# Transposing x into spare columns of the value banks, with a new order of loads and of work, in a fused window-attention and highway-layer kernel

## The chip, the cores and the metric

The kernel runs on one core of one Trainium2 chip. The metric is the device time of one execution in microseconds (us). Every timing below is a set of executions on one chip, with the kernel before run on the same chip in the same rounds. An execution is called slow when it is over 1.5% above the fastest of its kernel. The span of the profile is some 2 us shorter than the time of the same execution, so spans are compared with spans and times with times.

## The reference, cut to what matters

```python
# q, k, v: (4 batches, 8 heads, 768 positions, 64); first 4 positions are sinks, window of 128
scores = scale * q @ k.T
keep   = (pos_k < 4) | (0 <= pos_q - pos_k < 128)
a      = softmax(where(keep, scores, -1e9))
x      = (a @ v), heads side by side          # 3072 tokens x 512
H      = max(x @ w_h, 0)
T      = sigmoid(x @ w_t + b_t)
out    = T * H + (1 - T) * x
```

## The kernel before

The 3072 tokens are 24 blocks of 128. For each block TensorE does these steps, whose names are those of the order string further down: `S`, the scores (with the transposes of a later block's q and k ahead of them); `sk`, the scores against the four sinks, for one block or for two at once; `A`, the attention sums; `X`, the transposes of the result x; `Mh` and `Mt`, the two matrix products of the highway layer (hidden and gate). ScalarE does exp (`x0_`, `x1_`, `es`), tanh (`u`) and copies (`tq`, `tk`, `xT`). VectorE masks (`m0_`, `m1_`), normalises (`xh`) and combines (`d`, `e`, `o`); a `V` at the end of a copy's name means that VectorE does it. A step's place in the string is its place in the queue of its engine.

The accumulator memory has 8 banks: two tiles of two banks for scores (`s_ps`), one tile of two banks for attention sums, the value banks (`av_ps`), and two single work banks (`m_ps`), which `sk`, `X`, `Mh` and `Mt` take in turn.

```python
s_ps  = tc.tile_pool(name="ps_s",  bufs=2, space=PSUM)
av_ps = tc.tile_pool(name="ps_av", bufs=1, space=PSUM)
m_ps  = tc.tile_pool(name="ps_m",  bufs=2, space=PSUM)
...
def av_tile(n):
    if n not in av_of:
        av_of[n] = av_ps.tile([P, 2, 4, P], FP32, tag="av", name="av")   # 66 of each 128 columns used
    return av_of[n]
...
def pe_X(n):
    xh = xh_of[n]
    xtp = m_ps.tile([P, NOC, P], FP16, tag="m", name="xtp")              # a work bank
    for j in range(NOC):
        nc.tensor.transpose(xtp[:, j, :], xh[:, j * P:(j + 1) * P], ident)
    xtp_of[n] = xtp

def act_X(n, eng=None):
    xT = x_pool.tile([P, NOC, P], FP16, tag="xT", name="xT")
    (eng or nc.scalar.copy)(out=xT, in_=xtp_of.pop(n))
    xT_of[n] = xT
...
def pe_O(n):                                   # the sum of the last blocks' output, by TensorE
    ops = m_ps.tile([P, DM], FP32, tag="m", name="ops")
    nc.tensor.matmul(ops, lhsT=ident2, rhs=xh_of.pop(n), start=True, stop=False)
    nc.tensor.matmul(ops, lhsT=ident, rhs=ee_of.pop(n), start=False, stop=True)
    t_of[n] = ops
...
# GpSimd's queue of loads that cast to fp16
load_q(1); load_q(2); load_q(3); load_k(2)
...                                            # two small operations for a mask
load_k(4); load_k(3); load_v(2); load_w(moe_w_h, wh_sb); load_k(5); load_v(3)
load_w(moe_w_t, wt_sb); load_q(4); load_q(5)
...
ORDER = """
...
Mh:10 x1_:13 xh:12 Mt:11 tq:15 d:10 tk:15 m1_:13 X:12 u:11 S:14 xTV:12
e:10 A:13 x0_:14 o:10 Mh:11 x1_:14 xh:13 Mt:12 tq:16 d:11 tk:16 m0_:14 X:13 u:12 m1_:14 S:15
xT:13 e:11 sk:15 x0_:15 o:11 A:14 es:15 ...
...
"""
```

The softmax here doesn't subtract the row's maximum and nothing guards it: scores larger than these inputs give would overflow.

## Time and profile before

| | before |
|---|---|
| first timing, median of 3 runs | 126.18 us (126.16 to 127.13) |
| profiled execution | 126.71 us, span 124.6 us, granted TensorE clock 1.00 |
| TensorE busy | 112.2 us, 90% of the span |
| VectorE, ScalarE busy | 102.0 us, 91.5 us |

TensorE is the bound, VectorE comes next. I read a block's place in time from where its score step begins, that is from the first matmul of line 323, which has the same line in both kernels.

### The profile page before, as it was taken

To read this page: it belongs to the slowest core of one execution; us is meant where nothing else is said; L and a number is where in the kernel's file an instruction comes from. 1 tells how busy PE (TensorE), PEld (TensorE's weight loads), DVE (VectorE), ACT (ScalarE), POOL (GpSimd) and SP (SyncE) were. 2 spreads that over 40 slices of the span, in tenths; PEclk is the share of its full clock that TensorE was granted. 3 is DMA by queue.
4 is the path that set the end of the run, shared out by engine and by line. 5 is a ranking of instruction groups with operands and counts; after the bars stand their busy time and mean duration, and the time that the engine had idled before them with its cause. 6 is when DMAs were issued, how large, how long until landed. Compare 5 with 4: busy or idle time off the path is not lost.

```text
span 124.6 us, 4770 instructions
## 1 busy us (share of the span) xinstructions
PE 112.2 (90%) x2016; PEld 69.2 (56%) x2016; DVE 102.0 (82%) x239; ACT 91.5 (73%) x153; POOL 73.1 (59%) x97
## 2 busy tenths in 40 slices
PE   5958588999999979999999999999999999998950
PEld 1323356556675645766666666655665676663620
DVE  6855253889978999989998999799999999993970
ACT  2156478578899948889889699888798897953260
POOL 5998957799697899999599999642000000000000
PEclk9999999999999999999999999999999999999999
DMA  3999999999999999999999999996022211012044
GB/s 75 199 166 152 181 179 182 158 152 119 188 193 171 189 170 179 185 155 169 189 223 134 195 154 205 196 183 152 5 89 84 84 63 34 35 49 84 5 170 166
DMA packets 79847, 17.65 MB, mean 142 GB/s; under 512 B 75601, under 2 KB 76881, under 8 KB 79826
## 3 DMA queue, kind: packets, MB, share of 16 engines
q0 software_dynamic: 71888, 9.97, 127.1%
q1 hardware_dynamic: 6882, 7.11, 18.9%
q10 hardware_dynamic: 1056, 0.26, 1.3%
q8 instruction: 16, 0.26, 0.9%
q14 instruction: 5, 0.04, 0.1%
HBM read 21.01 MB, written 6.29 MB: 219 GB/s over the span
## 4 chain that ended last, share of the span: by engine, by line
PE 63%; DVE 20%; DMA 6%; issue 3%; POOL 2%; ACT 2%; DVEq 0%
PE tps L419 12%; PE hps L432 11%; DMA ksd<-in_k_dram 6%; PE av L378 6%; PE av L367 5%; DVE e L349 5%; PE sps L280 5%; DVE xh L397 4%; PE sps L323 4%; PE sps L336 4%; PE xtp L406 4%; PE tps L417 3%; PE sk L305 3%; PE av L384 3%; DVE ee L444 3%; DVE dd L438 3%
## 5 line engine op out<-in xcount | busy, mean ns | idle before, releaser
L341 ACT ACTIVATE e<-sps,ebias 128x768 f16<-128x768 f32 x48 | 41.1, 894 | 9.0 <-PE sps L336 9.0
L349 DVE TENSOR_TENSOR e<-e,mask 128x768 f16<-128x768 f16 x48 | 26.3, 570 | 4.4 <-ACT e L341 3.9
L285 ACT COPY t<-sps 128x512 f16<-128x512 f16 x45 | 24.1, 582 | 3.1 <-PE sps L280 3.1
L104 POOL DMA_DIRECT2D v<-in_v_dram x26 | 22.3, 860 | 5.9 <-DVE e L349 2.2
L432 PE MATMUL hps<-wh_sb,xT 128*128 128x512 f16 x92 | 23.4, 379 | 0.3 <-ACT u L425 0.3
L419 PE MATMUL tps<-wt_sb,xT 128*128 128x512 f16 x92 | 23.6, 379 | 0.0
L97 POOL DMA_DIRECT2D ksd<-in_k_dram x26 | 22.6, 874 | 0.4 <-issue 0.4
L90 POOL DMA_DIRECT2D qsd<-in_q_dram x23 | 21.4, 933 | 1.5 <-DMA qsd<-in_q_dram 1.2
L425 ACT ACTIVATE u<-tps 128x512 f16<-128x512 f32 x23 | 13.7, 597 | 7.3 <-PE tps L419 6.6
L397 DVE TENSOR_TENSOR xh<-av,rec 128x512 f16<-128x512 f32 x24 | 16.6, 692 | 0.8
L438 DVE SCALAR_TENSOR_TENSOR dd<-hps,xh 128x512 f16<-128x512 f32 x23 | 15.7, 688 | 1.8 <-PE hps L432 1.8
L444 DVE SCALAR_TENSOR_TENSOR ee<-u,dd 128x512 f16<-128x512 f16 x23 | 15.8, 687 | 0.8 <-ACT u L425 0.2
L450 DVE SCALAR_TENSOR_TENSOR otok<-xh,ee 128x512 f32<-128x512 f16 x20 | 14.5, 726 | 0.5
L419 PEld LDWEIGHTS <-xT 128*128 128x128 f16 x92 | 9.0, 98 | 9.8 <-issue 0.2
L432 PEld LDWEIGHTS <-xT 128*128 128x128 f16 x92 | 8.7, 98 | 7.6 <-issue 0.7
L323 PE MATMUL sps<-t,t 64*128 64x128 f16 x192 | 12.0, 217 | 0.2 <-ACT t L285 0.2
L367 PE MATMUL av<-v,e 64*64 64x66 f16 x384 | 10.9, 193 | 0.3 <-issue 0.2
L406 PE MATMUL xtp<-ident,xh 128*128 128x128 f16 x96 | 9.2, 219 | 2.0 <-DVE dd L438 1.0
L406 PEld LDWEIGHTS <-xh 128*128 128x128 f16 x96 | 6.8, 98 | 7.0 <-DVE xh L397 2.5
L378 PE MATMUL av<-v,e 128*128 128x66 f16 x192 | 10.4, 195 | 0.0
L392 DVE RECIPROCAL rec<-av 128x8 f32<-128x8 f32 x24 | 4.9, 204 | 5.9 <-PE av L384 5.2
L367 PEld LDWEIGHTS <-e 64*64 64x64 f16 x384 | 8.4, 107 | 1.9 <-issue 0.8
(84 smaller groups left out, 148.8 us busy)
## 6 DMA issues: line engine op xcount, KB each, us to landing
out_dram<-otok SPq DMA_DIRECT2D x23, 256.0 KB, 5.1
qsd<-in_q_dram POOLq DMA_DIRECT2D x23, 128.0 KB, 6.8
ksd<-in_k_dram POOLq DMA_DIRECT2D x19, 128.0 KB, 7.0
v<-in_v_dram POOLq DMA_DIRECT2D x19, 128.0 KB, 7.1
wh_sb<-in_moe_w_h_dram POOLq DMA_DIRECT2D x1, 512.0 KB, 8.1
wt_sb<-in_moe_w_t_dram POOLq DMA_DIRECT2D x1, 512.0 KB, 9.2
ksd<-in_k_dram POOLq DMA_DIRECT2D x7, 64.0 KB, 7.7
v<-in_v_dram POOLq DMA_DIRECT2D x7, 64.0 KB, 6.7
```

The lines of the kernel that those rows point to most:

```text
L90: nc.gpsimd.dma_start(out=qsd, in_=q[b, :, c * P:(c + 1) * P, :].transpose([1, 0, 2]))
L97: nc.gpsimd.dma_start(out=ksd[rows], in_=k[b, :, s0:s0 + nr, :].transpose([1, 0, 2]))
L104: nc.gpsimd.dma_start(out=vt[rows, :, 0:D], in_=v[b, :, s0:s0 + nr, :].transpose([1, 0, 2]))
L285: (eng or nc.scalar.copy)(out=t.rearrange("p a (h b) -> p h a b", b=HP), in_=t_view(s_tile(n, g), isinstance(n, tuple) and n[1:] in F32_T))
L341: nc.scalar.activation(out=e.rearrange("p a b c -> p a (b c)"), in_=s_tile(n, g)[:, :, 0:2 * EW], func=AF.Exp, bias=ebias, scale=SCALE)
L349: nc.vector.tensor_tensor(out=ev, in0=ev, in1=m.unsqueeze(1).to_broadcast([P, 4, EW]), op=ALU.mult)
L367: nc.tensor.matmul(av[part, h // 4, h % 4, 0:_AVN], lhsT=e_at(n, h)[src, P:EW], rhs=vt[src, 65 * h:65 * h + _AVN], start=(h % 4 == 0), sto ...
L397: nc.vector.tensor_tensor(out=xh.rearrange("p (h d) -> p h d", d=D), in0=av_of.pop(n)[:, :, 0:D], in1=rec_of.pop(n).unsqueeze(2).to_broadc ...
L406: nc.tensor.transpose(xtp[:, j, :], xh[:, j * P:(j + 1) * P], ident)
L419: nc.tensor.matmul(tps, lhsT=xT[:, kc, :], rhs=wt_sb[:, kc, :], start=False, stop=(kc == NOC - 1))
L432: nc.tensor.matmul(hps, lhsT=xT[:, kc, :], rhs=wh_sb[:, kc, :], start=(kc == 0), stop=(kc == NOC - 1))
L444: nc.vector.scalar_tensor_tensor(out=ee, in0=u_of.pop(n), scalar=1.0, in1=dd_of.pop(n), op0=ALU.add, op1=ALU.mult)
```

## The change

Its intent, in four parts.

1. x is transposed with eight transposes of 64 rows, into columns of the value banks that the attention sums leave unused. The work banks then serve `sk`, `Mh` and `Mt` alone.
2. A new order of the middle: the gate product before the hidden one, sink scores mostly behind the attention step, copies of x mostly on ScalarE.
3. A new start: another order of loads, made for the times at which they land, and another order of work.
4. A new tail, in which VectorE does all output sums.

```diff
-        load_q(1)
-        load_q(2)
         load_q(3)
         load_k(2)
+        load_q(4)
+        load_q(1)
+        load_k(3)
+        load_q(2)
+        load_v(2)
+        load_k(5)
 ...
         load_k(4)
-        load_k(3)
-        load_v(2)
+        load_v(3)
         load_w(moe_w_h, wh_sb)
-        load_k(5)
-        load_v(3)
-        load_w(moe_w_t, wt_sb)
-        load_q(4)
         load_q(5)
         load_k(6)
+        load_w(moe_w_t, wt_sb)
 ...
+    def x_view(n):
+        return av_t[n].bitcast(FP16)[:, :, :, 2 * _AVN:2 * _AVN + HP]
+
     def pe_X(n):
         xh = xh_of[n]
-        xtp = m_ps.tile([P, NOC, P], FP16, tag="m", name="xtp")
+        xv = x_view(n)
         for j in range(NOC):
-            nc.tensor.transpose(xtp[:, j, :], xh[:, j * P:(j + 1) * P], ident)
-        xtp_of[n] = xtp
+            for hf in range(2):
+                rows = slice(HP * hf, HP * hf + HP)
+                nc.tensor.transpose(xv[:, hf, j, :], xh[rows, j * P:(j + 1) * P],
+                                    ident[rows, rows])
 ...
-        (eng or nc.scalar.copy)(out=xT, in_=xtp_of.pop(n))
+        (eng or nc.scalar.copy)(out=xT.rearrange("p a (h b) -> p h a b", b=HP), in_=x_view(n))
 ...
-    H0 = 4
+    H0 = 3
 ...  (ORDER: all lines; two blocks of the middle)
-    Mh:10 x1_:13 xh:12 Mt:11 tq:15 d:10 tk:15 m1_:13 X:12 u:11 S:14 xTV:12
-    e:10 A:13 x0_:14 o:10 Mh:11 x1_:14 xh:13 Mt:12 tq:16 d:11 tk:16 m0_:14 X:13 u:12 m1_:14 S:15
-    xT:13 e:11 sk:15 x0_:15 o:11 A:14
+    u:10 X:12 S:14 d:11 xT:12 e:10 A:13 x0_:14 o:10 Mt:11 x1_:14
+    xh:13 tq:16 Mh:12 tk:16 m0_:14 u:11 m1_:14 X:13 S:15 d:12 xT:13 e:11 A:14 x0_:15 o:11 sk:15
```

More of the change, by code (lines that the diff above doesn't have):

```diff
@@ L211 @@
         load_q(7)
-        load_v(7)
         load_v(6)
         load_v(8)
+        load_v(7)
     def first_mask(_):
@@ L256 @@
     qT, kT, s_of, e_of, av_of, rec_of, es_of = {}, {}, {}, {}, {}, {}, {}
-    xtp_of, xh_of, xT_of, t_of, u_of, h_of, dd_of, ee_of, sk_of = {}, {}, {}, {}, {}, {}, {}, {}, {}
+    av_t, xh_of, xT_of, t_of, u_of, h_of, dd_of, ee_of, sk_of = {}, {}, {}, {}, {}, {}, {}, {}, {}
     def s_tile(n, g):
@@ L357, in av_tile @@
             av_of[n] = av_ps.tile([P, 2, 4, P], FP32, tag="av", name="av")
+            av_t[n] = av_of[n]
         return av_of[n]
@@ L400, in dve_x @@
         xh_of[n] = xh
+    def x_view(n):
+        return av_t[n].bitcast(FP16)[:, :, :, 2 * _AVN:2 * _AVN + HP]
     def pe_X(n):
         xh = xh_of[n]
-        xtp = m_ps.tile([P, NOC, P], FP16, tag="m", name="xtp")
+        xv = x_view(n)
         for j in range(NOC):
-            nc.tensor.transpose(xtp[:, j, :], xh[:, j * P:(j + 1) * P], ident)
-        xtp_of[n] = xtp
+            for hf in range(2):
+                rows = slice(HP * hf, HP * hf + HP)
+                nc.tensor.transpose(xv[:, hf, j, :], xh[rows, j * P:(j + 1) * P],
+                                    ident[rows, rows])
     def act_X(n, eng=None):
         xT = x_pool.tile([P, NOC, P], FP16, tag="xT", name="xT")
-        (eng or nc.scalar.copy)(out=xT, in_=xtp_of.pop(n))
+        (eng or nc.scalar.copy)(out=xT.rearrange("p a (h b) -> p h a b", b=HP), in_=x_view(n))
+        av_t.pop(n)
         xT_of[n] = xT
@@ L587 @@
     ORDER = """
-    ma:0 mz0_:0 na:0 Tk:0 na:1 mz1_:0 tk:0 wA:0 Tk:1 ma:1 Tq:0 tk:1 fa:0 tq:0 cv:0 cv:1 wA:0
-    wA:0 wA:0 Tq:1 tq:1 fc:0 wA:0 wA:0 S:0 mc:0 x0_:0 fb:0 fd:0 x1_:0 wA:0 wA:0 wA:0 wA:0 wA:0
-    Tk:2 m0_:0 tk:2 Tq:3 m1_:0 tq:3 wA:0 wA:0 S:1 x0_:1 x1_:1 wA:0 wA:0 wA:0 wA:0 Tk:3 m0_:1
-    sk:3 tkV:3 sk:1 es:3 m1_:1 A:0 es:1 Tq:2 xh:0 tq:2 X:0 sk:2 xT:0 S:2 es:2 A:1 x0_:2 Mh:0
-    x1_:2 xh:1 m0_:2 X:1 Tk:4 m1_:2 xT:1 Tk:5 d:0 tk:4 A:2 tk:5 Mh:1 xh:2 S:3 d:1 X:2 x0_:3 Mt:0
-    xTV:2 x1_:3 m0_:3 Tq:4 u:0 Mt:1 m1_:3 tq:4 e:0 sk:4 o:0 u:1 S:4 es:4 e:1 Mh:2 x0_:4 o:1
@@ L594 @@
-    x1_:4 A:3 d:2 tq:5 m0_:4 Mt:2 tk:6 xh:3 S:5 m1_:4 u:2 e:2 X:3 x0_:5 A:4 xTV:3 x1_:5 m0_:5
-    sk:5 Mt:3 xh:4 es:5 tq:6 m1_:5 tk:7 X:4 o:2 u:3 S:6 xT:4 A:5 x0_:6 Mh:3 x1_:6 xh:5 Mt:4 tq:7
-    d:3 tk:8 m0_:6 X:5 u:4 m1_:6 S:7 xT:5 e:3 A:6 x0_:7 o:3 Mt:5 x1_:7 xh:6 Mh:4 u:5 m0_:7 tq:8
-    m1_:7 d:4 tk:9 sk:7 Tq:9 e:4 es:7 X:6 tq:9 Mh:5 xTV:6 o:4 S:8 d:5 A:7 x0_:8 e:5 Mt:6 o:5
-    x1_:8 xh:7 tq:10 Mh:6 tk:10 m0_:8 u:6 m1_:8 S:9 d:6 A:8 x0_:9 e:6 X:7 x1_:9 sk:9 xTV:7 xh:8
-    Mt:7 es:9 tq:11 m0_:9 tk:11 X:8 m1_:9 u:7 S:10 xTV:8 o:6 A:9 x0_:10 Mh:7 x1_:10 xh:9 Mt:8
@@ L600 @@
-    tq:12 d:7 tk:12 m0_:10 X:9 u:8 m1_:10 S:11 xT:9 e:7 sk:11 x0_:11 o:7 A:10 es:11 m0_:11
-    x1_:11 Mh:8 xh:10 tq:13 Mt:9 d:8 tk:13 m1_:11 X:10 u:9 S:12 xTV:10 e:8 A:11 x0_:12 o:8 Mh:9
-    x1_:12 xh:11 Mt:10 tq:14 d:9 tk:14 m0_:12 X:11 u:10 m1_:12 S:13 xT:11 e:9 sk:13 x0_:13 o:9
-    A:12 es:13 m0_:13 Mh:10 x1_:13 xh:12 Mt:11 tq:15 d:10 tk:15 m1_:13 X:12 u:11 S:14 xTV:12
-    e:10 A:13 x0_:14 o:10 Mh:11 x1_:14 xh:13 Mt:12 tq:16 d:11 tk:16 m0_:14 X:13 u:12 m1_:14 S:15
-    xT:13 e:11 sk:15 x0_:15 o:11 A:14 es:15 m0_:15 x1_:15 Mh:12 xh:14 tq:17 Mt:13 d:12 tk:17
@@ L606 @@
-    m1_:15 X:14 u:13 e:12 S:16 xT:14 o:12 A:15 x0_:16 Mh:13 x1_:16 xh:15 Mt:14 tq:18 d:13 tk:18
-    m0_:16 X:15 u:14 m1_:16 S:17 xT:15 e:13 sk:17 x0_:17 o:13 A:16 es:17 m0_:17 x1_:17 Mh:14
-    xh:16 tq:19 Mt:15 d:14 tk:19 m1_:17 X:16 u:15 S:18 xTV:16 e:14 A:17 x0_:18 o:14 Mh:15 x1_:18
-    xh:17 Mt:16 tq:20 d:15 tk:20 m0_:18 X:17 u:16 m1_:18 S:19 xT:17 e:15 sk:19 x0_:19 o:15 A:18
-    es:19 m0_:19 Mh:16 x1_:19 xh:18 Mt:17 tq:21 d:16 tk:21 m1_:19 X:18 u:17 S:20 xTV:18 e:16
-    A:19 x0_:20 o:16 Mh:17 x1_:20 xh:19 Mt:18 tq:22 d:17 tk:22 m0_:20 X:19 u:18 m1_:20 S:21
@@ L612 @@
-    xT:19 e:17 A:20 x0_:21 o:17 sk:21 x1_:21 xh:20 Mh:19 es:21 m0_:21 tq:23 Mh:18 m1_:21 tk:23
-    d:19 S:22 d:18 A:21 x1_:22 e:18 sk:23 x0_:22 Mt:19 xh:21 tk:24 m0_:22 es:23 S:23 m1_:22 u:19
-    o:18 X:21 x0_:23 X:20 xTV:21 A:22 xT:20 m0_:23 x1_:23 Mt:21 xh:22 m1_:23 Mh:20 u:21 e:19
-    X:22 d:20 A:23 xT:22 o:19 Mt:22 xh:23 u:22 X:23 xT:23 Mh:21 Mh:22 d:21 Tb:23 e:21 Ta:23 d:22
-    ub:23 Hb:23 ua:23 e:22 Mt:20 db:23 eb:23 O:22 u:20 pb:23 Ha:23 oc:22 e:20 O:21 da:23 oc:21
-    O:20 ea:23 oc:20 pa:23
+    mz0_:0 ma:0 na:0 Tq:0 na:1 Tk:0 tq:0 mz1_:0 tk:0 ma:1 wA:0 wA:0 Tk:1 mc:0 cv:0 tk:1 fa:0
@@ new lines @@
+    wA:0 wA:0 wA:0 S:0 cv:1 x0_:0 fb:0 x1_:0 wA:0 wA:0 wA:0 wA:0 Tq:3 m0_:0 tq:3 wA:0 Tk:2 m1_:0
+    tk:2 fc:0 fd:0 wA:0 wA:0 wA:0 wA:0 wA:0 Tq:1 A:0 tq:1 S:1 xh:0 sk:1 x0_:1 x1_:1 Tq:2 m0_:1
+    X:0 sk:3 xTV:0 es:1 Tk:3 m1_:1 tq:2 tk:3 wA:1 A:1 es:3 S:2 xh:1 x0_:2 x1_:2 Tk:4 m0_:2 sk:2
+    tkV:4 X:1 es:2 m1_:2 S:3 xT:1 A:2 x0_:3 Mh:1 x1_:3 xh:2 tq:4 d:1 X:2 Mh:0 xT:2 m0_:3 tk:5
+    m1_:3 Mh:2 d:0 S:4 d:2 Mt:0 x0_:4 x1_:4 m0_:4 A:3 u:0 m1_:4 Mt:1 tq:5 xh:3 tk:6 sk:4 e:0 u:1
+    S:5 es:4 o:0 X:3 x0_:5 sk:5 xTV:3 e:1 A:4 x1_:5 m0_:5 Mt:2 tq:6 xh:4 tk:7 es:5 m1_:5 X:4 u:2
@@ new lines @@
+    S:6 xTV:4 o:1 A:5 x0_:6 e:2 Mh:3 x1_:6 xh:5 Mh:4 tq:7 m0_:6 tk:8 m1_:6 X:5 S:7 d:3 xT:5 d:4
+    A:6 x0_:7 o:2 Mh:5 x1_:7 xh:6 Mt:3 tq:8 d:5 tk:9 X:6 m0_:7 u:3 Mt:5 m1_:7 xT:6 e:3 sk:7 u:5
+    o:3 Tq:9 es:7 Mt:6 e:5 tq:9 o:5 u:6 S:8 A:7 x0_:8 Mh:6 x1_:8 xh:7 tq:10 m0_:8 X:7 tk:10
+    m1_:8 sk:9 xT:7 d:6 S:9 es:9 e:6 A:8 x0_:9 o:6 Mt:7 x1_:9 xh:8 tq:11 Mt:4 m0_:9 tk:11 m1_:9
+    u:7 X:8 u:4 S:10 xTV:8 e:4 A:9 x0_:10 o:4 Mh:8 x1_:10 xh:9 Mh:7 tq:12 m0_:10 tk:12 m1_:10
+    X:9 S:11 xT:9 d:8 A:10 d:7 x0_:11 sk:11 e:7 x1_:11 Mt:8 xh:10 es:11 tq:13 Mh:9 o:7 tk:13 u:8
@@ new lines @@
+    m0_:11 X:10 S:12 xT:10 m1_:11 d:9 A:11 x0_:12 e:8 Mt:9 x1_:12 xh:11 tq:14 Mh:10 m0_:12 tk:14
+    m1_:12 u:9 X:11 d:10 S:13 xT:11 o:8 A:12 x0_:13 e:9 sk:13 x1_:13 xh:12 Mt:10 es:13 m0_:13
+    tq:15 Mh:11 m1_:13 tk:15 o:9 u:10 X:12 S:14 d:11 xT:12 e:10 A:13 x0_:14 o:10 Mt:11 x1_:14
+    xh:13 tq:16 Mh:12 tk:16 m0_:14 u:11 m1_:14 X:13 S:15 d:12 xT:13 e:11 A:14 x0_:15 o:11 sk:15
+    x1_:15 Mt:12 xh:14 es:15 tq:17 m0_:15 Mh:13 tk:17 m1_:15 u:12 X:14 d:13 S:16 xT:14 e:12 A:15
+    x0_:16 o:12 Mt:13 x1_:16 xh:15 tq:18 Mh:14 m0_:16 tk:18 m1_:16 u:13 X:15 d:14 S:17 xT:15
@@ new lines @@
+    e:13 A:16 x0_:17 o:13 sk:17 x1_:17 Mt:14 xh:16 es:17 tq:19 m0_:17 Mh:15 tk:19 m1_:17 u:14
+    X:16 d:15 S:18 xT:16 e:14 A:17 x0_:18 o:14 Mt:15 x1_:18 xh:17 tq:20 Mh:16 m0_:18 tk:20
+    m1_:18 u:15 X:17 d:16 S:19 xT:17 e:15 A:18 x0_:19 o:15 sk:19 x1_:19 Mt:16 xh:18 es:19 m0_:19
+    tq:21 Mh:17 m1_:19 tk:21 u:16 X:18 d:17 S:20 xT:18 e:16 A:19 x0_:20 o:16 Mt:17 x1_:20 xh:19
+    tq:22 Mh:18 m0_:20 u:17 m1_:20 tk:22 sk:21 d:18 X:19 es:21 S:21 xTV:19 e:17 A:20 x0_:21 o:17
+    Mt:18 x1_:21 xh:20 tq:23 Mh:19 m0_:21 u:18 m1_:21 tk:23 X:20 d:19 sk:23 xT:20 S:22 e:18
@@ L618 @@
+    es:23 A:21 x1_:22 o:18 Mt:19 x0_:22 xh:21 tk:24 m0_:22 X:21 xT:21 m1_:22 S:23 u:19 A:22
+    x0_:23 e:19 Mh:20 xh:22 x1_:23 Mh:21 d:20 m0_:23 X:22 Mt:21 xT:22 m1_:23 d:21 A:23 o:19 u:21
+    e:21 Mh:22 xh:23 Mt:22 d:22 o:21 X:23 u:22 Mt:20 xT:23 e:22 Tb:23 o:22 u:20 Ta:23 ub:23 e:20
+    Ha:23 ua:23 o:20 Hb:23 da:23 db:23 ea:23 eb:23 pa:23 pb:23
     """
```

## The prediction

> **What bounds the kernel now.** I read the page first, then the chain that ended last, then the timeline of one block and of both ends.
>
> ```profile
> PE 112.2 (90%) x2016; PEld 69.2 (56%) x2016; DVE 102.0 (82%) x239; ACT 91.5 (73%) x153; POOL 73.1 (59%) x97
> PE   5958588999999979999999999999999999998950
> PE 63%; DVE 20%; DMA 6%; issue 3%; POOL 2%; ACT 2%; DVEq 0%
> ```
>
> TensorE (PE) is busy almost without a break from slice 8 (about 25 us) to slice 37, and it holds 63% of the chain. VectorE is not far behind: 4.6 to 4.9 us of each 5 us from 55 to 110. So I cut the run into a start (until the score step of block 4, at 28.7 us), a PE-bound middle of 19 blocks, and a tail. The chain gives the rhythm of the middle; columns are start, length, work:
>
> ```profile
> 54.42 0.25 PE sps L336 x16
> ...
> 58.25 0.25 PE sps L336 x16
> ...
> 62.53 0.25 PE sps L336 x16
> ```
>
> A block without sink scores takes 58.25 - 54.42 = 3.83 us, the next one, with four sink matmuls, 4.28; one with eight takes 4.50 (74.93 to 79.43). Inside a block, from the timeline (start, modelled length, work):
>
> ```profile
> 57.30 0.39 PE L406 MATMUL xtp<-ident,xh 128*128 128x128 f16 x4
> 57.62 0.29 PE L280 MATMUL sps<-ident,qsd 64*128 64x64 f16 x8
> 57.75 0.28 PE L323 MATMUL sps<-t,t 64*128 64x128 f16 x4
> ...
> 58.18 0.32 PE L336 MATMUL sps<-t,t 64*64 64x64 f16 x16
> ...
> 58.43 0.40 PE L305 MATMUL sk<-t,ks 128*128 128x128 f16 x4
> ...
> 58.76 0.45 PE L367 MATMUL av<-v,e 64*64 64x66 f16 x16
> ...
> 59.14 0.43 PE L378 MATMUL av<-v,e 128*128 128x66 f16 x8
> ```
>
> Only differences of starts count, since matmuls overlap. Four full transposes of x hold PE 0.32 us (57.30 to 57.62); the eight 64-row transposes of q hold it 0.13. Sink scores wedged between the score step and the attention step stretch those three starts to 0.25, 0.33 and 0.38; in the block before, without them, the same stretch was 0.16 and 0.35. That is 0.45 us for four matmuls of 0.056.
>
> The start is held by loads and by order:
>
> ```profile
> 5.60 7.99 DMA ksd<-in_k_dram
> 13.63 0.31 PE sps L280 x8
> ...
> 117.50 0.88 PE tps L419 x4
> 118.40 0.60 ACT u L425
> 119.03 0.69 DVE ee L444
> ```
>
> Key chunk 2 is the fourth load in GpSimd's queue and lands 8 us after its issue. The last lines are the tail: the final gate matmul ends, then ScalarE and a row of small VectorE steps until 120.98.
>
> **What the Trainium skill says.** "TensorEngine Tiling (Array Packing)", Key Properties: changing the tiling mode drains TensorE, and different tiles can work in parallel. The trace agrees: each change of mode shows some 0.1 us more than the plain spacing (four matmuls of L323 last 0.11 us, then 0.21 passes before L336 starts), and eight transposes over two row tiles take 0.13 us. "PSUM — Partial Sum Buffer", the section on bank collisions: two engines must not touch one bank and quadrant at once, even in other columns. So x in spare columns does not free the value banks early; they stay closed until x has been copied out. No trace here shows a collision. "DMA: Bandwidth & Descriptors", SWDGE vs HWDGE vs iDMA: a load that casts must be issued by GpSimd. The trace agrees in that all fp32-to-fp16 loads are there, at 0.86 to 0.93 us of GpSimd each, so their order is the order of landing.
>
> **Part 1, x transposed in the value banks.** Removed: 24 times four 128-row transposes into the pool of two work banks. Added: 24 times eight 64-row ones. The number of mode changes stays (the change now falls ahead of x instead of after it). Gain on PE: 0.32 - (0.13 + 0.09 for the change) = 0.10 us a block. It also empties the two work banks of one user, which before made PE wait 1.0 us on VectorE's dd in all. The cost: there is one value tile only. Before, the next attention step waited for the normalisation alone; now it waits for the copy of x to SBUF too. From the start of the transposes (zero): change 0.09, issue 0.13, last result some 0.2 later (that modelled latency is in every row), copy on ScalarE 0.58, release 0.05, so attention may start at about 1.05. PE has 0.22 + 0.72 = 0.94 us of transposes and scores in between (q to attention, 53.79 to 54.51). I put the wait at 0.13 us a block. So a plain block is a wash: 3.83 - 0.10 + 0.13 = 3.86.
>
> **Part 2, the order of the middle.** Sink scores mostly move from between scores and attention to behind attention, where the mode is 128 anyway. That saves 0.45 - 0.22 = 0.23 us in each of about 9 such blocks, 2 us. Gate matmuls (Mt) move ahead of the hidden ones (Mh), so tanh runs beside Mh and ScalarE is free when x comes. Copies of x go from VectorE to ScalarE nearly everywhere (ten on VectorE before, five after): VectorE loses 5 x 0.42 = 2.1 us. ScalarE then needs about 1.59 + 0.97 + 0.50 + 0.49 = 3.55 us a block by starts (two exps, two copies, tanh, x), plus 0.4 with sinks, below PE.
>
> Sum of PE's middle, score step 4 to score step 23. Before: 19 scores of 0.72, 19 attentions of 0.86, 18 x of 0.31, 18 Mh of 0.86, 18 Mt of 1.08, 68 sink matmuls of 0.056 and 1.8 for their mode changes make 76.1; the trace has 106.55 - 28.69 = 77.9, so 1.8 is stalls. After: the same scores and attentions (30.0), 19 x of 0.22 (4.2), 17 Mh (14.7), 20 Mt (21.6), sinks 3.8, sum 74.3; with 19 waits of 0.13 (2.5) and 1.0 of other stalls 77.8. Two gate matmul groups more and one hidden group less are left to this stretch than before (1.3 us); so for equal work it gains 1.4.
>
> **Part 3, the start.** In the order before, PE's queue puts the transpose of q 1 (which waits for a load until 9.62) ahead of score step 0 (10.39). Now score step 0 needs the early fp32 loads only, the last transposed at 7.05 to 7.5 and copied by about 8.1: it starts near 8.2. q 1 is now the fourth load, issued near 5.6, so it lands where key chunk 2 landed, 13.1 to 13.6, and score step 1 stays near 14.3 (14.5 before). But attention 0 is then already done (17.3 before), and key 3, q 2, v 2 come directly behind at 0.9 us each instead of behind key 4 and 1 MB of weights. From there by durations: exps of block 1 to 16.7, masks 17.3, attention 1 to 18.2, score step 2 at 18.2 (19.74), score step 3 near 20.0 (25.10), attention 2, then Mh 1, 0 and 2, score step 4 near 25.2 (28.69). That is 3.5 earlier, minus 1.3 for the work moved to the middle: 2.2 net.
>
> **Part 4, the tail.** Three output sums by PE (6 x 0.22 = 1.3 us) and three copies on ScalarE go; three sums of 0.73 go to VectorE. From the end of score step 23 PE has two attentions 1.9, three Mh 2.6, three Mt 3.2, x 0.5, four half groups 2.1: 10.3, against 12.0 before (107.3 to 119.3). VectorE then needs about 0.2 + six halves of 0.35: end near 12.6 after score step 23, against 13.7. Gain 1.1.
>
> **Sum.** Score step 4 at 25.2, middle 77.8, step 0.72, tail 12.6: 116.3 against 121.0 for the same point before. Gain 4.7 (2.2 + 1.4 + 1.1), so 126.18 - 4.7 = 121.5.
>
> **Rivals.** (a) The copy of x takes back more: if ScalarE is late by another 0.15 us a block, 19 blocks lose 2.9 us and the time is near 124.4. For it: one value tile, ScalarE already at 3.55 of 3.86. Against it: attention loses its wait only if ScalarE has work ahead of x, and with Mt first, tanh ends about 0.3 us before x is transposed. (b) VectorE becomes the bound. By starts a block needs 0.61 (sum) + 0.86 (norm) + 0.61 + 0.93 + 0.61 = 3.62; over the middle that is 70 of 78 us, so it can trail PE but not hold it; if its waits line up badly, 123. (c) The early loads are bound by the transfers, not by their order (the first 15 us run at 126 to 168 GB/s): the start then gains 1 instead of 2.2, 122.7. (d) The hidden x wait is nil because PE is late anyway: 119.5.
>
> **Range and chances.** My guess of the errors is 1.5 us for the start, 1.8 for the middle and 0.5 for the tail; taken as independent that is 2.4, a generous one, of which I use 2.0 each way for eight times in ten. Range 119.6 to 123.6. Two per cent is 123.66, so faster 0.89, same 0.1, slower 0.01.
>
> **What would show it.** Right: the x transposes at 64*128 with eight in about 0.13 us; score step 0 near 8.2 and score step 4 near 25; blocks near 3.86 without and 4.1 to 4.3 with sinks, sinks behind attention; a PE wait for the copy of x ahead of L367 of some 0.1 us; no rows of lines 459 to 465. Wrong: that wait at 0.3 or more, score step 1 after 15.5, VectorE above 97% in the middle, or slower spacing of the 64-row x transposes.

## More of the kernel before

One more line is used later: the longest wait of TensorE that lies in the middle of the run, from the view of waits (who waited, for whom, us in total, times, longest).

```profile
engine line waited for: us in total, times, longest us
...
PE xtp L406 <- DVE dd L438: 1.0, 2, 0.7
```

The transposes of x waited twice for VectorE to read a work bank empty.

## The result, and the profile after

| | before | after |
|---|---|---|
| median, same chip, 4 runs each | 126.64 us (126.16 to 127.13) | 122.71 us (122.38 to 123.2) |
| profiled execution | 126.71 us, span 124.6 | 122.54 us, span 120.5, clock 0.996 |

The change is faster: the ratio is 0.969, with a 95% interval of 0.963 to 0.976. The gain by medians is 3.9 us. A ratio here is the mean time of one kernel's fast runs over that of the other's in the same rounds, so it is not quite the ratio of the medians. That matters for the experiments: on their chips the kernel before scattered from 124.2 to 128.2 us, the mean of its fast runs lies up to 1.2 us under its median, and so the ratios look a little worse for a kernel than the medians do. I give both.

The page of the changed kernel: busy time, TensorE's busy share in 40 slices, and the share of the last chain by engine.

```profile
PE 109.2 (91%) x2105; PEld 66.0 (55%) x2105; DVE 103.1 (86%) x237; ACT 92.7 (77%) x155; POOL 73.7 (61%) x97
...
PE   5999696999999999997999999989999999999920
...
PE 57%; DMA 18%; POOL 7%; DVE 6%; issue 4%; ACT 4%; DVEq 0%; ACTq 0%; POOLq 0%
```

TensorE is still the bound. Its first seven slices (some 21 us) read 5, 9, 9, 9, 6, 9, 6, where before they read 5, 9, 5, 8, 5, 8, 8. The larger DMA share of the chain is no new bound: the chain happened to be followed through GpSimd's loads of q instead of through TensorE's queue in the stretch from 22 to 40 us, where TensorE is busy in every slice.

Where the 4.1 us of the spans came from, by the first score matmul (L323) of a block:

| | before | after | gain |
|---|---|---|---|
| score step 0, 1, 2, 3 begin at | 10.39, 14.60, 19.74, 25.03 | 8.10, 13.58, 17.53, 20.03 | |
| score step 4 | 28.82 | 24.91 | 3.91 |
| score step 8 | 46.36 | 43.73 | 2.63 |
| score step 23 | 106.55 | 103.79 | 2.76 |
| end of the span | 124.6 | 120.5 | 4.1 |

At score step 4 the changed kernel has done less gate and hidden work than the old one. At score step 8 both have done the same twelve groups, so 2.63 us is the true lead of the start. From there to score step 23 the middle takes 60.19 us before and 60.06 us after: it gained 0.1 us. The tail gained 1.3 us. One thing is not equal at this cut: by the order strings the changed kernel transposes x of blocks 20 and 21 ahead of score step 23, the old one behind it. At 0.23 us each (the two figures below) that is some 0.5 us more work in the new middle, an estimate, so for equal work the middle gained some 0.6 us. What the tail is worth for equal work is read from experiment 12. (The prediction cut at score step 4 and took off 1.3 us for the work that was moved: 3.91 - 1.3 = 2.6 for the start, and 77.73 - 78.88 + 1.3 = 0.15 for the middle, the same.)

One block of the middle, from TensorE's timeline of the changed kernel (start, modelled length, work, count):

```profile
62.50 1.03 PE L439 MATMUL hps<-wh_sb,xT 128*128 128x512 f16 x4
63.46 0.29 PE L412 MATMUL av<-ident,xh 64*128 64x64 f16 x8
63.59 0.28 PE L280 MATMUL sps<-ident,qsd 64*128 64x64 f16 x8
63.70 0.28 PE L323 MATMUL sps<-t,t 64*128 64x128 f16 x4
...
64.14 0.32 PE L336 MATMUL sps<-t,t 64*64 64x64 f16 x16
64.43 0.35 PE L368 MATMUL av<-v,e 64*64 64x66 f16 x11
```

The eight transposes of x (L412) hold TensorE for 63.59 - 63.46 = 0.13 us. The hidden product takes 0.86 us of issue, so the change of mode ahead of them costs 63.46 - 62.50 - 0.86 = 0.10. From the last score group to the attention (L336 to L368) there is 0.29 us; before it was 0.16 in a block without sinks. The extra 0.13 us is the wait until x has been copied out of the value banks. A block without sinks takes 3.88 us (score step 12 to 13 and 14 to 15), one with eight sink matmuls behind the attention 4.33 (15 to 16).

The start, from the chain (start, length, work), has one load in it that counts, that of q 1:

```profile
5.60 6.96 DMA qsd<-in_q_dram
12.61 0.29 PE sps L280 x8
```

And the tail, from the same chain:

```profile
110.96 0.88 PE tps L426 x4
...
111.92 0.61 ACT u L432
112.55 0.70 DVE ee L451
113.27 0.69 DVE otok L457
...
116.71 0.34 DVE otok L515
```

The chain leaves TensorE near 111.8, with the gate product of block 22, and from 112.55 VectorE works its row almost without a break to 117.4. TensorE goes on beside it: its last full gate product, that of block 20, ends near 113.2, its last matmul near 115.2. Before, the chain left TensorE only at 118.4.

What the middle lost shows in TensorE's waits, and in its timeline at two places:

```profile
engine line waited for: us in total, times, longest us
...
PE sps L336 <- issue: 1.4, 2, 0.8
```

```profile
55.15 0.32 PE L336 MATMUL sps<-t,t 64*64 64x64 f16 x15
56.31 0.19 PE L336 MATMUL sps<-t,t 64*64 64x64 f16 x1 [0.84 <-issue]
...
80.34 0.25 PE L336 MATMUL sps<-t,t 64*64 64x64 f16 x6
81.13 0.28 PE L336 MATMUL sps<-t,t 64*64 64x64 f16 x10 [0.54 <-issue]
```

TensorE stops in the middle of a group of 16 equal matmuls, for which everything was ready, and goes on later. "issue" says that the profile shows nothing for which it waited. Score step 11 to 12 takes 5.10 us and 17 to 18 takes 4.76; in a run in which these two blocks were undisturbed (experiment 7) they took 4.11 and 4.10. So the two pauses cost 1.0 + 0.65 = 1.65 us.

The kernel before has such pauses too, again inside groups of equal matmuls:

```profile
67.17 0.45 PE L305 MATMUL sk<-t,ks 128*128 128x128 f16 x5 [0.29 <-issue]
...
80.00 0.35 PE L367 MATMUL av<-v,e 64*64 64x66 f16 x10 [0.23 <-issue]
```

Score step 13 to 14 takes 4.73 us there and 16 to 17 takes 4.24; in experiment 5, where the old order ran without a pause in these blocks, they took 4.27 and 3.83. So they cost 0.46 + 0.41 = 0.87 us. Without the pauses of either kernel the stretch from score step 8 to 23 would take 59.3 us before and 58.4 after.

VectorE did not hold the middle, as a table of busy time from 60 to 80 us shows (first before, then after; us of the window, then busy us and instructions of PE, PEld, DVE, ACT and POOL, then granted clock, DMA share and GB/s):

```profile
60.00:80.00 20.00, 19.48 (x389) 12.46 (x386) 18.90 (x36) 17.36 (x30) 18.79 (x23) 1.00 2.04 180
```

```profile
60.00:80.00 20.00, 20.00 (x433) 12.60 (x429) 18.58 (x36) 19.16 (x33) 18.21 (x24) 1.00 2.00 182
```

VectorE went from 18.90 to 18.58 us of 20, ScalarE from 17.36 to 19.16, as copies of x moved to it.

### The profile page after: what moved, and what is told of

It is laid out like the page before. It is cut to its first block, busy times and chain, and to the rows that moved or that the text cites.

```text
span 120.5 us, 4964 instructions
## 1 busy us (share of the span) xinstructions
PE 109.2 (91%) x2105; PEld 66.0 (55%) x2105; DVE 103.1 (86%) x237; ACT 92.7 (77%) x155; POOL 73.7 (61%) x97
## 4 chain that ended last, share of the span: by engine, by line
PE 57%; DMA 18%; POOL 7%; DVE 6%; issue 4%; ACT 4%; DVEq 0%; ACTq 0%; POOLq 0%
DMA qsd<-in_q_dram 18%; PE tps L426 11%; PE hps L439 11%; PE av L368 6%; PE av L379 5%; PE sps L336 4%; PE sps L323 4%; PE sps L280 4%; PE sk L305 3%; PE tps L424 3%; ACT e L341 3%; PE av L385 3%; PE av L412 3%; POOL qsd L90 2%; POOL ksd L97 2%
## 5 line engine op out<-in xcount | busy, mean ns | idle before, releaser
L349 DVE TENSOR_TENSOR e<-e,mask 128x768 f16<-128x768 f16 x48 | 24.8, 550 | 2.4 <-ACT e L341 2.4
L451 DVE SCALAR_TENSOR_TENSOR ee<-u,dd 128x512 f16<-128x512 f16 x23 | 17.2, 748 | 0.9 <-ACT u L432 0.7
L457 DVE SCALAR_TENSOR_TENSOR otok<-xh,ee 128x512 f32<-128x512 f16 x23 | 15.8, 689 | 0.6
L417 ACT COPY xT<-av 128x512 f16<-128x512 f16 x19 | 11.2, 587 | 2.1 <-PE av L412 2.0
L323 PE MATMUL sps<-t,t 64*128 64x128 f16 x192 | 11.9, 217 | 0.1
L368 PEld LDWEIGHTS <-e 64*64 64x64 f16 x384 | 9.3, 107 | 3.0 <-issue 1.2
L368 PE MATMUL av<-v,e 64*64 64x66 f16 x384 | 10.8, 193 | 0.2 <-DVE xT L417 0.2
L336 PE MATMUL sps<-t,t 64*64 64x64 f16 x384 | 8.0, 198 | 1.4 <-issue 1.4
```

What stands on the lines that cost most here:

```text
L323: nc.tensor.matmul(sps[:, hh, hl * EW:hl * EW + P], lhsT=kT[n][rows, hp, :], rhs=qT[n][rows, hp, :], start=True, stop=True)
L349: nc.vector.tensor_tensor(out=ev, in0=ev, in1=m.unsqueeze(1).to_broadcast([P, 4, EW]), op=ALU.mult)
L368: nc.tensor.matmul(av[part, h // 4, h % 4, 0:_AVN], lhsT=e_at(n, h)[src, P:EW], rhs=vt[src, 65 * h:65 * h + _AVN], start=(h % 4 == 0), sto ...
L451: nc.vector.scalar_tensor_tensor(out=ee, in0=u_of.pop(n), scalar=1.0, in1=dd_of.pop(n), op0=ALU.add, op1=ALU.mult)
```

## The experiments

All twelve kernels gave correct results. Each was run six times, among the runs of the kernel before (eleven on each chip). Profiled executions were fast unless I say slow. Against 2%, experiments 1 and 3 are slower, 2, 4, 9 and 11 the same, and 5 to 8, 10 and 12 unclear, among them the changed kernel itself (10). So differences of 1% between these kernels are read from the traces and not from the times. Seven of the kernels change the changed kernel; five graft a part of the change onto the old one. The theory was the prediction's: the new x is a wash in time, the start gives 2.2 us, the order of the middle 1.4 and the tail 1.1.

### 1. The changed kernel with the old x

```diff
-        xv = x_view(n)
+        xtp = m_ps.tile([P, NOC, P], FP16, tag="m", name="xtp")
         for j in range(NOC):
-            for hf in range(2):
-                ...
+            nc.tensor.transpose(xtp[:, j, :], xh[:, j * P:(j + 1) * P], ident)
```

> The changed kernel (new loads, new order), but x transposed as before: four 128-row transposes into the work banks. My theory: the new transpose is about a wash in itself, since its gain of 0.1 us a block is eaten by the wait of attention for the copy of x (0.15 us in the changed trace), so plain blocks go from 3.89 to about 3.83 us and the time stays within 0.7 us of the changed kernel (121.9 to 123.2). Rival: the worth of the change is that x no longer takes one of the two work banks; then gate and hidden matmuls wait for a bank again, and the time is 124 or more.

Measured: 133.08 us median, ratio 1.060 (1.055 to 1.065) against before, far slower than both kernels. The block of 3.88 us became 4.39. The timeline of the block around 67 us, and a line of the waits:

```profile
66.71 1.03 PE L433 MATMUL hps<-wh_sb,xT 128*128 128x512 f16 x4
...
67.45 0.63 ACT L426 ACTIVATE u<-tps 128x512 f16<-128x512 f32 x1
68.13 0.38 PE L407 MATMUL xtp<-ident,xh 128*128 128x128 f16 x4 [0.40 <-ACT u L426]
```

```profile
PE xtp L407 <- ACT u L426: 3.2, 9, 0.4
```

With the gate product first, the gate takes one work bank, the hidden product the other, and x needs the first one again: it must wait until tanh has read it, and tanh ends at 68.08. In the old order the hidden product went first, and its bank was free when x came, but for the two waits shown above. The block is 0.5 us longer, and the stretch from score step 4 to 23 takes 87.55 us against 78.88: that is most of the 10 us by which this kernel is slower than the changed one (it is 7 us slower than the kernel before). So the new x is no wash in the new order. My expectation fell, the rival was right.

### 2. The changed kernel with the old order of loads

```diff
-        load_q(3), load_k(2), load_q(4), load_q(1), load_k(3), load_q(2), load_v(2), load_k(5), ...
+        load_q(1), load_q(2), load_q(3), load_k(2), ..., load_k(4), load_k(3), load_v(2), ...
```

(The two lines are shortened; q 4 comes after both weights again.)

> The changed kernel with GpSimd's loads in the order of before. My theory: about a third of the gain at the start comes from the loads: score step 1 waits for key chunk 2 until 13.6 again (it started at 13.57 with q 1 at 12.6), score step 4 starts about 1 us later than 24.8, and the time is near 123.6. Rival A: the whole start gain of 3 to 4 us hangs on the loads, 125 or more. Rival B: the transfers are bound by throughput and only the order of TensorE's work matters, 122.6 as the changed kernel.

Measured: 127.56 us median, ratio 1.007 (1.000 to 1.014); the profile is a slow one, clock 0.967. Score step 1 begins at 16.44 instead of 13.58, score step 4 at 28.00 instead of 24.91. The waits show which load it is:

```profile
PE sps L280 <- DMA qsd<-in_q_dram: 2.8, 2, 2.5
```

The order of work of the new start needs q 3 and q 4 early, and alone, without its order of loads, it loses 3.1 us; rival A's number came. Some 1.1 us of this is the clock: after a wait of 2.5 us for q 3 the granted clock was 0.50 from 12.3 to 15.7 us, and five matmuls ahead of q 1 that only keep TensorE busy (`wA`) took 2.3 us there, by their modelled lengths, instead of 1.25. Score step 23 is another 2.8 us later, and 2.7 of that lie in one block, score step 11 to 12, which took 7.79 us: a pause of 2.2 us, then half clock (see experiment 11). Its fast runs had a clock of only 0.97 as well, so they have such stretches too; whether the order of loads lengthens that pause stays open.

### 3. The kernel before with the new x alone

```diff
-  ... X:3 x0_:5 A:4 xTV:3 ...        +  ... X:3 x0_:5 xTV:3 A:4 ...
-  ... A:8 x0_:9 e:6 X:7 x1_:9 ...    +  ... X:7 xTV:7 A:8 x0_:9 e:6 x1_:9 ...
```

(And the same for the last blocks. Four copies had to go ahead of the next attention, which now needs the value banks back.)

> The kernel before (its loads, its order, its tail) with the new transpose of x alone; the transpose or copy of x of blocks 3, 7, 20 and 22 had to move ahead of the next attention. My theory: without the new order ScalarE still has tanh ahead of the copy of x, so attention waits 0.3 us in half of the blocks: 1 to 2.5 us slower than before, about 128. Rival: shorter transposes and freed work banks are where the gain comes from, then faster than before by 2 us or more (124.5).

Measured: 130.06 us median, ratio 1.031 (1.024 to 1.039). A block takes 4.15 to 4.2 us instead of 3.83.

```profile
PE av L368 <- ACT xT L417: 2.8, 7, 0.7
PE av L368 <- DVE xT L417: 2.4, 4, 0.8
```

In the old order tanh stands ahead of the copy of x on ScalarE, and on VectorE other work does, so attention waits 5.2 us in all for the value banks. I expected a loss here, and the loss was larger than I had said. Experiments 1 and 3 together, by medians: everything but the new place of x is 7 us slower than the kernel before, the new place of x alone 4 us, and only together do they keep a block at 3.88 us.

### 4. The kernel before with the sinks behind the attention

```diff
-  xT:13 e:11 sk:15 x0_:15 o:11 A:14 es:15
+  xT:13 e:11 x0_:15 o:11 A:14 sk:15 es:15      (the same for 11, 13, 17, 19)
```

> The kernel before with the sink scores of blocks 11, 13, 15, 17 and 19 moved from between scores and attention to behind attention, nothing else. My theory: each saves two changes of tiling mode, 0.23 us, so 5 x 0.23 = 1.15 us, a ratio near 0.991, and periods of 4.27 instead of 4.50 for eight sink matmuls. Rival: ScalarE or VectorE takes the slack and the time does not move (ratio 0.998 to 1.002).

Measured: 126.48 us median, ratio 1.006 (1.000 to 1.012): the same time as before. The profile is a slow one with the full clock. Three of the five blocks can be read cleanly: score step 11 to 12 went from 4.28 to 4.17 us, 15 to 16 from 4.50 to 4.28, 19 to 20 from 4.27 to 4.23. Of the other two, 13 to 14 holds a pause, and 17 to 18, with 4.88 us against 4.76, saved nothing: attention waited 0.25 us there for VectorE's mask. The second pause lies in 16 to 17:

```profile
PE av L367 <- issue: 1.7, 2, 0.9
```

So there is a local saving, 0.04 to 0.22 us in three blocks, much too small to be seen in the whole. The time did not move, as the rival said.

### 5. The new start on the old kernel, joined at score step 4

The loads and the order of the changed kernel up to score step 4, with the new x for blocks 0 to 2; the old order from there.

> The changed kernel's loads and order up to score step 4 (x of blocks 0 to 2 in the value banks), and from there every remaining step in the order of before, with x in the work banks as before, and the old tail with its sums by TensorE. My theory now: the start carries most of the gain, 2.6 us of work done earlier (3.9 us earlier at score step 4, less 1.3 us of work that is still to do), so a ratio near 0.980. Rival: the middle of before, which relied on the older start, loses it again to waits and the ratio is above 0.99.

Measured: 126.44 us median, ratio 1.012 (1.005 to 1.018), unclear. Score step 3 begins at 20.55, as in the changed kernel, and score step 4 at 29.69, later than before. The joint itself is at fault: two gate products follow one another there, and each waits for tanh.

```profile
27.32 0.38 PE L443 MATMUL tps<-bt,ones_row 128*128 128x512 f16 x1 [0.69 <-ACT u L451]
...
29.25 0.38 PE L306 MATMUL sk<-t,ks 128*128 128x128 f16 x4 [0.69 <-ACT u L451]
```

At that step this kernel has also done one hidden product (0.86 us) more than the kernel before, so for equal work the lead was nil. My number was missed. This says nothing on the worth of the start. I made the joint again in experiment 9.

### 6. The new tail on the old kernel

The order of the changed kernel from score step 23 on, x of blocks 21 to 23 in the value banks.

> The kernel before with the changed kernel's order from score step 23 on (no sums by TensorE, x of blocks 21 to 23 in the value banks). Theory: the tail by itself is worth what the two traces show from score step 23 to the last VectorE instruction, 14.4 against 13.6, so about 0.85 us, a ratio near 0.993. Rival: VectorE, which takes three more sums of 0.69 us, eats it: ratio 0.998 or more.

Measured: 125.24 us median against 126.13 of before, ratio 1.004 (0.997 to 1.011), unclear. By medians it gains 0.9 us, by fast runs nothing. In the trace the stretch from score step 22 to the end takes 20.57 us against 20.90 before and 19.48 in the changed kernel. The graft had to put two extra transposes of x ahead of score step 23, so it is no clean copy of the tail: score step 22 to 23 took 3.72 us instead of 2.85. The ratio is the rival's, but whether VectorE's sums are the reason is not shown. Experiment 12 takes the other direction.

### 7. The changed kernel with 128-row transposes into the same columns

```diff
-            for hf in range(2):
-                rows = slice(HP * hf, HP * hf + HP)
-                nc.tensor.transpose(xv[:, hf, j, :], xh[rows, j * P:(j + 1) * P], ident[rows, rows])
+            nc.tensor.transpose(xv[:, j // 2, 2 * (j % 2):2 * (j % 2) + 2, :],
+                                xh[:, j * P:(j + 1) * P], ident)
```

> The changed kernel with x transposed in four 128-row transposes, into the same spare columns of the value banks and at the same places in the order. By the prediction's own count this costs TensorE 0.1 us a block, 2 us in all (ratio 0.985). My theory now: attention does not start when TensorE is free but when the copy of x is out, and the last transpose of x ends at the same time in both forms (0.09 mode change and eight in 0.13, against four in 0.22), so the time is that of the changed kernel within 0.4 us, ratio 0.966 to 0.973.

Measured: 123.24 us median, ratio 0.985 (0.976 to 0.993). A block without sinks takes 3.88 us, the same as with the 64-row pairs. The timeline says why:

```profile
63.45 0.39 PE L410 MATMUL av<-ident,xh 128*128 128x128 f16 x4
63.77 0.29 PE L280 MATMUL sps<-ident,qsd 64*128 64x64 f16 x8
...
64.33 0.32 PE L336 MATMUL sps<-t,t 64*64 64x64 f16 x16
64.51 0.45 PE L368 MATMUL av<-v,e 64*64 64x66 f16 x16
```

The four large transposes hold TensorE 0.32 us instead of 0.23 with the change of mode, so attention could start that much later; but now it starts 0.18 us after the last score group instead of 0.29. What the small transposes save is given back at the wait for the copy. Some other blocks are longer with the large ones (score step 6 to 7, 9 to 11, 13 to 14, 19 to 21 by some 0.1 us each, 5 to 6 and 22 to 23 by 0.2 to 0.3), about 1 us in all. So my expectation (0.966 to 0.973) was missed by some 1%: it is a wash in the plain blocks only. The pauses at score steps 11 and 17 are gone in this program; one of 1.27 us stands in the attention step of 16 to 17 instead, which took 5.33 us.

### 8. The same, with x between the gate and the hidden product

`X` moved ahead of `Mh` for blocks 10 to 18 and 20, to give the copy of x more time.

> As e7, and in ten blocks of the middle (10 to 18 and 20) x is transposed between the gate and the hidden matmuls instead of behind both, so that the copy of x is out before attention wants the banks. If the wait for the copy is what the blocks lose, ten blocks gain about 0.1 us each and the time is 0.5 to 1 us under e7. Rival: the normalised x is not ready by the end of the gate matmuls (VectorE), then TensorE waits there instead and the time is that of e7 or up to 2 us more.

Measured: 124.28 us median, ratio 0.995 (0.986 to 1.003). From score step 13 to 20 blocks take 4.2 to 4.5 us: x is not normalised yet when TensorE comes to it.

```profile
PE av L410 <- DVE xh L398: 1.3, 6, 0.3
```

The rival was right: the room on that side is VectorE's, and it has none.

### 9. The new start on the old kernel, joined at score step 6

> e5 with a better seam: the changed kernel's loads and order up to score step 6, where only one gate group less is done than in the order before, then the steps of before. e5 lost its lead between score steps 3 and 4, where both gate groups had to share a bank with ScalarE and VectorE idle. Theory: without that the start keeps 2.6 us of the gain, about two thirds of the whole: a median 2 to 2.6 us under that of before (ratio 0.979 to 0.984), score step 8 near 44.2 instead of 46.8. Rival: the order of before in the middle cannot keep the lead; score step 8 comes at 46 or later and the gain is under 1 us.

Measured: 125.85 us median against 126.25 of before, ratio 1.003 (0.997 to 1.010). Score step 3 begins at 21.25, 1.2 us later than in the changed kernel (a stretch of half clock in this profile, 15.5 to 18.9 us), score step 6 at 35.51 and score step 8 at 45.77, against 36.29 and 46.36 before. At score steps 6 and 8 it has done the same gate and hidden products as the kernel before, so a lead of 0.8 us was left at the joint and 0.6 at score step 8. (The lead of nearly 4 us at score step 3 is in part work left for later.) The rival's numbers came; but most of the lead was lost ahead of the joint, so its reason, that the old order cannot keep the lead, is not shown. Neither joint therefore gives the start's worth alone; the 2.6 us are read from the two traces, and experiment 2 shows that they hang on the order of loads.

### 10. The changed kernel again

No edit; another chip, and a second profile.

> The changed kernel unchanged, beside the others on one chip, for comparison and for a second trace. Expected: 122.4 to 123.2, ratio 0.965 to 0.977. If the two pauses of TensorE in the middle of a run of small matmuls (1.04 us near 55.5 and 0.74 near 80.6) come from the program, they stand at the same steps again; if they come from a late fetch of instructions, they follow a packet of the instruction queue by 1 to 2 us and may stand elsewhere or have another length.

Measured: 122.67 us median (121.33 to 126.19), ratio 0.974 (0.967 to 0.982). Its profile is a slow one, span 122.3, clock 0.989. The pauses come at the same two score steps, 11 and 17, ahead of the same matmul of the sixteen; the first of them:

```profile
56.39 0.32 PE L336 MATMUL sps<-t,t 64*64 64x64 f16 x15
57.81 0.19 PE L336 MATMUL sps<-t,t 64*64 64x64 f16 x1 [1.11 <-issue]
```

A third one, of 0.54 us at 37.5 us, the first profile does not have. Their place is set by the program; their length (1.9 us for the two by the view of waits here, 1.4 in the first profile), and whether one appears, by the run.

### 11. The changed kernel with q 1 and key 2 loaded first

```diff
-        load_q(3); load_k(2); load_q(4); load_q(1); load_k(3); ...
+        load_q(1); load_k(2); ...                          (and S:1 ahead of A:0)
```

> The changed kernel with q 1 and key 2 as the first two loads, q 3 and key 4 transposed beside score step 2 (they were separate steps), and the order up to score step 3 rewritten for that. The changed kernel waits for q 1, its fourth load, until 12.6. If the start is bound by which load comes when, score step 1 comes near 12 instead of 13.9, score step 4 1 to 1.5 us earlier, and the time is 1 to 1.5 us under the changed kernel. Rival: weights or value chunk 3 land too late for the earlier start, and at score step 4 or 5 nothing is left of it.

Measured: 125.02 us median, ratio 0.991 (0.983 to 1.000); the profile is a slow one. Score step 1 begins at 11.80, 1.8 us earlier, score step 2 at 16.79, score step 4 at 24.96, which is no lead any more. q 1 holds score step 1 alone. By score step 4 nothing is left, as the rival said; which loads or exps take it was not taken apart. Against the changed kernel on this chip (0.974) it even loses 1.7%; in this profile that comes from pauses, in score steps 5 to 6 (4.65 us), 11 to 12 and 17 to 18 (5.43).

This profile shows a cost of pauses that I had not reckoned with: here one of 1.6 us fell into the attention step after score step 11 (the waits put it down to a VectorE row that ended then, though the first of the 16 matmuls of the group had already run), and then the granted clock fell. From the table of busy time in steps of 1 us (columns as above):

```profile
57.00:58.00 1.00, 0.21 (x13) 0.21 (x14) 0.43 (x1) 0.76 (x1) 0.43 (x2) 1.00 2.22 205
58.00:59.00 1.00, 1.00 (x29) 0.93 (x21) 0.16 (x1) 0.00 (x0) 1.00 (x2) 0.85 1.69 254
59.00:60.00 1.00, 1.00 (x5) 0.45 (x4) 0.97 (x3) 0.76 (x3) 0.80 (x2) 0.50 2.40 156
...
62.00:63.00 1.00, 1.00 (x29) 0.56 (x29) 0.32 (x1) 0.09 (x1) 1.00 (x2) 0.94 2.34 161
```

For over 3 us TensorE ran at half clock. The block took 7.55 us instead of 4.11, so this pause of 1.6 us cost 3.4.

### 12. The changed kernel with the old tail

The changed kernel up to score step 23, then the old order with the sums by TensorE and x of blocks 22 and 23 in the work banks.

> The changed kernel up to score step 23, and from there the steps of before: three output sums by TensorE and their copies by ScalarE, x of blocks 22 and 23 in the work banks. By the two traces the tail from score step 23 to the end is worth 1.5 us (17.6 before, 16.1 after). If that is so, this one ends 1 to 1.5 us later than the changed kernel: 17.2 to 17.6 us from score step 23 to the end of the span, a median 1 to 1.5 us above it. Rival: the tail's gain came from the middle's order leading into it, then this one is within 0.4 us of the changed kernel.

Measured: 125.16 us median, ratio 0.983 (0.972 to 0.994) from only two fast runs; the profile is a slow one. From score step 23 to the end it takes 17.87 us, against 16.75 in experiment 10's profile (slow as well) and 16.71 and 18.05 in the two profiles of after and before. Against the changed kernel the work left at score step 23 is the same here, so for equal work the new tail is worth 1.1 to 1.2 us in the trace.

No version beats the changed kernel clearly. The nearest, with the large transposes, is 0.985 with an interval that overlaps that of the changed kernel on the same chip (0.974, 0.967 to 0.982).

## Why the prediction was right, point by point

The prediction said 121.5 us, 119.6 to 123.6, and faster by over 2% with a chance of 0.89. It came out at 122.71 us, 3.1% faster. The gain was 3.9 us instead of 4.7. That it came so near is in part luck: the start gave 0.4 us more, and the last store an unpredicted 0.5, against 1.3 too little in the middle. Term by term, in spans, cut as the prediction cut them:

| term | predicted | measured |
|---|---|---|
| start (net of work moved to the middle) | 2.2 | 2.6 |
| middle, for equal gate and hidden work | 1.4 | 0.1 |
| tail | 1.1 | 1.3 |
| sum | 4.7 | 4.1 |

**The start was right.** Score steps 0, 2, 3 and 4 began within 0.7 us of what was said (8.10, 17.53, 20.03 and 24.91 against 8.2, 18.2, 20.0 and 25.2), and q 1, the fourth load, does hold score step 1: it landed at 12.6 instead of 13.1 to 13.6, so that score step 1 began at 13.58 instead of 14.3. The 0.4 us that the start gained beyond the prediction are 0.3 of its score step 4 and 0.1 of the old one's, which I had read at 28.69, at the transposes that precede it. Rival (c), that the transfers and not their order hold the start, fell with experiment 2.

**Part 1, x, was right in its sizes and too narrow in its reading.** 0.10 us less on TensorE, 0.13 us of wait, a block of 3.86: measured were 0.13 for the transposes, 0.10 for the change of mode, 0.13 of wait and 3.88. Experiment 7 shows the wash in the plain blocks. But I had treated it as a wash in any order. Experiments 1 and 3 show that x and the order are one change: the order needs the work banks free of x, and x in the value banks needs the tanh ahead of its copy to have ended, which the gate-first order provides. That is also why rival (a), 0.15 us more of wait per block, did not come: with the old order it came in full and more (5.2 us).

**Part 2, the order of the middle, is the term that was mis-sized.** Two steps of it failed. "0.23 us in each of about 9 such blocks" was a miscount: before, only five sink steps of the middle stood between scores and attention (11, 13, 15, 17 and 19), and experiment 4 measured 0.04 to 0.22 us for three of them. At their mean, 0.12, five blocks give at most 0.6 us, an estimate, instead of 2. The rest of those 2 us must then have been other stalls of the old kernel, and I had assumed that the new one would have only "1.0 of other stalls". It has the two pauses, 1.65 us, and a wait of 0.3 us for GpSimd to write sink keys (score step 7 to 8 took 7.17 us against 6.87 where that wait was absent, in experiments 2 and 11). That is 0.95 us over what I had allowed, and the middle from score step 4 to 23 took 78.88 us where I had said 77.8: 1.1 over. The old kernel had pauses as well (0.87 us). Without those of either kernel the order gained 0.9 us from score step 8 to 23 (59.3 to 58.4), the lost waits of x for VectorE's dd among it; 0.8 us of it was paid back in longer pauses. VectorE, rival (b), was busy 18.6 of 20 us and did not hold TensorE as a whole. Rival (d) fell with the 0.13 us. Two readings of the prediction were off without much weight: VectorE's busy time before was 4.0 to 4.9 us of each 5 us and not 4.6 to 4.9, and 17 steps X, not 18, lie between score steps 4 and 23; that the new order has two more of them there (20 and 21) was not taken off as moved work.

**The tail was right.** From the end of score step 23 to VectorE's last instruction it took 12.7 us (predicted 12.6, before 13.7). A further 0.5 us came from the last store, which landed sooner after it: 3.1 us from there to the end of the span instead of 3.6. I had not predicted that. Experiment 12 confirms the tail.

**What stays open is why the pauses come.** They are not a wait for data, since they split groups of matmuls that were all released together. Their end, however, goes with one thing in the traces: a packet of 16 KB in the queue that the profile page calls "instruction". Each run has 16 of these packets. The fourteen kept profiles have 28 pauses (27 that the timeline puts down to "issue", and that of 1.6 us in experiment 11), and in every one TensorE went on 1.2 to 1.7 us after the latest such packet had ended. In the changed kernel the packets lasted from 53.92 to 54.86 and from 78.65 to 79.53 us, and TensorE went on at 56.31 and 81.13. When the packet came later, the pause was longer: in experiment 2 it started only 0.2 us before the pause of 2.2 us. The third pause of experiment 10 followed a packet that ended at 36.09; in the first profile this packet had ended at 35.45, and there was no pause. So a late fetch of instructions fits, in where a pause ends and in how long it is. It is still argued from times and not shown: most packets are followed by no pause, no experiment here moved one on purpose, and what makes a packet late is not known.

## What to carry to other kernels

When a change moves a buffer and rewrites an order together, test each alone before you call one of them a wash: here x alone lost 4 us and the rest without it 7 us against the kernel before, and together they were neutral in the steady state and made the rest possible. When you add up the time of a rewritten order, carry over as many unexplained stalls as the old trace has, because a trace without them was never seen. And count the cases from the order itself, not from one good example: the 0.23 us was worked out from the block of score step 11, which then gained 0.11; of the other three that could be read one gained 0.22, one 0.04 and one nothing.

## What the Trainium skill lacked or had wrong

- "TensorEngine Tiling (Array Packing)", Key Properties, says that a change of tiling mode drains TensorE and gives no cost. Here one change costs 0.10 us (62.50 + 0.86 to 63.46).
- "TensorE: Matmul & The Clock Gate", What's actually happening, gives about 3.4 us idle before the clock falls to half. In experiment 11 it fell after a pause of 1.6 us, and stayed at 0.50 for over 3 us (some 58.7 to 62.1); after the pauses of 1.49 us in experiment 3 and 1.27 us in experiment 7 it did not fall.
- The same page, Part 4: PE-mode transpose, gives some 275 ns for a 128x128 transpose in a kernel and says that the full clock does not engage for it. The 96 such transposes of the kernel before averaged 219 ns by the profile's modelled lengths, as the score matmuls of 128 columns did (217 ns), in a run with the full clock granted in every slice.
- "Runtime: NRT & Kernel Launch", Instruction fetch mechanics, says that the cost of passing from one 16 KiB block of instructions to the next is mostly hidden, and names a stall for taken branches only. Here TensorE stopped inside groups of released matmuls, for 0.2 to 2.2 us by the timeline, and went on 1.2 to 1.7 us after a 16 KB packet of the instruction queue had ended, 28 times in fourteen profiles. That the fetch is the cause is argued and not shown.
